# Turning a local attention's sums on VectorE in the main loop instead of on TensorE between the output products

## The chip, the cores and the metric

The kernel runs on one core of a Trainium2 chip. The metric is the time of one execution on the device, in microseconds. The core has five engines that run side by side, each through its own list of instructions in the order in which they were written: TensorE (PE in the profile, its weight loads PEld), VectorE (DVE), ScalarE (ACT), GpSimd (POOL) and SyncE (SP), whose queue issues the DMA transfers. An instruction waits on semaphores until what it needs is there, and everything behind it on its engine waits too.

## The reference

Two attentions over the same input of 2048 rows by 448 features, 16 heads of 28, mixed by a gate per row. Shortened:

```python
g = sigmoid((x * gate_w).sum(-1, keepdims=True))
a = local(x, A_wqkv) @ A_wo      # each row looks at rows s, s-2, ..., s-14
b = full(x, B_wqkv) @ B_wo       # softmax over all 2048 rows
return g * a + (1 - g) * b
```

All in float32. To keep that precision at TensorE's faster float32 rate, the kernel writes each operand as a rounded part and a remainder (hi and lo) and adds three products: hi by hi, hi by lo, lo by hi.

## The kernel before

Rows are spread so that partition p holds rows 16p to 16p+15; "j" counts these 16.

First come the projections (q, k, v of both attentions). Then the main loop: 256 steps, 16 units (4 groups of four heads by 4 blocks of 512 queries) of 16 key tiles. In each step `scores` issues twelve score products (three terms for each of four heads) and two exponentials of 128x1024 on ScalarE; `do_av` then issues the products with V for the step before. Into the same steps is woven a search ahead for the largest score of each later query: three products of 512 keys a step (`s0`, `s1`, `s2`), whose maxima VectorE takes in two instructions, one over one bank (`s0`), one over two (`s1`, `s2`). The scores' banks rotate among three two-bank tiles: the tile that `s1` and `s2` fill in one step holds the third and the fourth head's scores in the next. The order of the products in a step is the string

```python
WITH = "10 20 s0 11 21 30 00 12 22 31 01 s1 s2 32 02".split()
```

in which "30" is the first term of the third head, the first product that needs that tile. The search has a head start from the projections and ends at step 234; in the last 21 steps there are no maxima.

The local attention runs beside it in 8 chunks of two heads, on GpSimd (products and sums), VectorE (reductions) and ScalarE (exponentials). It is not written in order: `item` puts each piece into a list with a key, a cost and its needs, each need with a lag in steps, and `issue` takes from an engine's list, in each step, what is due, as long as the engine's estimated lateness `late` plus the cost stays under a limit; for VectorE the limit is `DLIM`, 0.6 before. Each step takes 0.4 off VectorE's lateness while there are maxima. A reduction of local scores (`a_reduce`) has cost 0.32, those of the softmax 0.35. VectorE's items of a step are issued behind the step's two maxima.

The sum of a chunk is stored by rows into `oa_scr` (one transfer of 128x16x56). When all lists are empty, `a_done` sets off the first loads for the output products. These are 16 tiles of 128 rows. A tile multiplies 128 rows of both attentions' sums (seven slices of 128 features) with the output weights: 21 products of 448 columns (12 for the first tile, whose first nine are issued in the last step of the main loop). The full attention's sums are stored by feature and already split, so they load ready for use. The local sums come by row: `op_t` turns four 128x128 squares on TensorE for the tile that follows, and `op_split` splits them from the bank, on ScalarE and VectorE. Beside the first tiles runs the end of the full attention's last unit (`fin_...`, the list `steps`): sums stored and loaded, inverted, spread, multiplied, split, stored.

Of the kernel before, what the change touches and what calls it, by code (L numbers as in the profile page):

```python
# [8 lines left out]
F32 = mybir.dt.float32  # L9
# [16 lines left out]
def gated_mix_kernel(ctx: ExitStack, tc: tile.TileContext, xT, xn, gw, wA, wB, woAB, out):  # L26
# [9 lines left out]
    a_prev = [t[:, 0:S, :].rearrange("c (p j) e -> c p j e", j=NJ) for t in a_scr]  # L36
    oa_scr = dram.tile([128, NJ, D], F32, name="oa_scr")
    on_hi = dram.tile([D, S], F32R, name="on_hi")
# [134 lines left out]

    def max_parts(u):
# [8 lines left out]
        nc.gpsimd.tensor_tensor(out=t[:, 16:32], in0=v, in1=t[:, 0:16].bitcast(F32), op=ALU.subtract)  # L183
        return t
# [399 lines left out]
    for nme in ("k", "v"):  # L584
        for i in range(2):
            t = a1.tile([128, HALO + NJ, 56], F32, name=f"{nme}t{i}")
            kvt[nme, i] = t
    qt, Lt, oat, lst, prods = {}, {}, {}, {}, {}

# [26 lines left out]
    def a_softmax(c, i):  # L616
# [23 lines left out]
        else:  # L640
# [3 lines left out]
                [128, W, NJ * 2]), op=ALU.mult)  # L644

    def a_av(c, w, part):
        if part == 0:
# [31 lines left out]
    for c in range(8):  # L679
        c0 = CH * c - 5 * (c == 7)  # L680
        for nme in "qkv":
            item("sp", c0 if nme != "v" else c0 + 18, ("ld", nme, c), 0,
                 [(("s", c - 2, 7), 3)] if nme != "v" else [(("a", c - 2, 7, 1), 3)],
                 lambda c=c, nme=nme: a_load(c, nme))
        for w, o in enumerate((0, 2, 5, 8, 11, 14, 17, 20)):
            back = (c, w - 4) if w > 3 else (c - 1, w + 4)
            item("pool", c0 + o, ("s", c, w), 3.15 + 0.5 * (NR[c, w] == 1),
                 [(("ld", "k", c), 4), (("ld", "q", c), 4), (("a", c - 3, 7, 0), 0), (("s", c, w - 1), 0)]
                 + ([(last(*back), 0)] if back in NR else []), lambda c=c, w=w: a_score(c, w))
            for i in range(NR[c, w]):  # L690
# [3 lines left out]
        for i, (eng, o, cost, lag) in enumerate((("pool", 22, 0.68, 2), ("dve", 23, 0.35, 3), ("dve", 23.5, 0.35, 0),  # L694
                                                 ("pool", 25, 0.68, 1), ("act", 26, 0.3, 3), ("dve", 27, 0.35, 1),
                                                 ("dve", 27.5, 0.35, 0), ("dve", 27.8, 0.36, 0),
                                                 ("pool", 28, 0.9, 1))):
            item(eng, c0 + o, ("m", c, i), cost, [(last(c, 7) if i == 0 else ("m", c, i - 1), lag)],
                 lambda c=c, i=i: a_softmax(c, i))
        n = 0  # L700
        for w in range(W):
            for part in ((0,) if w == 0 else (0, 1)):
                item("pool", CH * c + 30 + 1.4 * n, ("a", c, w, part), 1.65 if part == 0 else 2.05,
                     [(("m", c, 8), 0), (("ld", "v", c), 4),
                      (("a", c, w - 1, 1 if w > 1 else 0) if part == 0 else ("a", c, w, 0), 0)],
                     lambda c=c, w=w, part=part: a_av(c, w, part))
                n += 1
    for q in lists.values():
        q.sort(key=lambda x: x[0])
# [22 lines left out]
    WO_AT = OP0 + 8  # L732
    A_START, DLIM, LOOK = 5, 0.6, 40

# [28 lines left out]

    oaT, onT = {}, {}

    def op_load_a(j):
        t = mtile("oal")
        nc.sync.dma_start(t[:, :D], oa_scr[:, j, :])
        oaT[j] = t

# [11 lines left out]

    def op_t(j):
        t = oaT[j]
        for k in range(4):
            n = 128 if k < 3 else 64
            writes(side["t"], nc.tensor.transpose(side["t"][0:n, 128 * k:128 * k + 128], t[:, 128 * k:128 * k + n], ident))  # L787

    def op_split(j):
        b, jj = divmod(j, 4)  # L790
        bank = side["t"]
        cs = slice(128 * jj, 128 * jj + 128)
        hi, lo = mtile("oah").bitcast(F32R), mtile("oalo").bitcast(F32R)
        th, tl = on_tiles(b)[0]
        nc.scalar.activation(hi[:, :384], bank[:, :384], AF.Copy)
        nc.scalar.activation(th[0:64, cs], bank[0:64, 384:512], AF.Copy)
        nc.vector.tensor_tensor(out=lo[:, :384], in0=bank[:, :384], in1=hi[:, :384].bitcast(F32), op=ALU.subtract)
        nc.vector.tensor_tensor(out=tl[0:64, cs], in0=bank[0:64, 384:512], in1=th[0:64, cs].bitcast(F32),
                                op=ALU.subtract)
        oaT[j] = (hi, lo)  # L800

    TERMS = ((0, 0), (0, 1), (1, 0))

    def op_mm(j, bank, ks, first=False, last=False):
        b, jj = divmod(j, 4)
        for k in ks:
            for i, (a, c) in enumerate(TERMS):
                src = oaT[j][a][:, 128 * k:128 * k + 128] if k < 3 else onT[b][k - 3][a][:, 128 * jj:128 * jj + 128]
                writes(bank, nc.tensor.matmul(bank[:, :D], src, wo[c][k],  # L809
# [89 lines left out]
    accs = []  # L899
    side = {}  # L900
# [36 lines left out]
    def scores(u, kt, cur):  # L937
# [9 lines left out]
        for tok in WITH if k else ALONE:  # L947
# [13 lines left out]
            if t == 2 and a in "20":  # L961
                if len(exps) < 8:
                    probs.append(pair("P"))
                p = probs[len(exps) % 8]
                e = nc.scalar.activation(p, one if a == "2" else mine, AF.Exp, scale=SCALE).ins  # L965
                for o in exps[-8:-7]:
                    tc.declare_no_dep(e, o, query=mybir.DependencyQuery.ANY_SYNC,
# [7 lines left out]
    for u in range(NU):  # L975
        g, b = divmod(u, NB)
        for kt in range(NJ):
# [18 lines left out]
            if finished:  # L996
                v = finished.pop(0)
                t = max_parts(v)
# [60 lines left out]
```

## Time and profile before

| | |
|---|---|
| median of 3 runs | 910.9 us (910.88 to 911.29) |
| the profiled execution | 911.58 us, span 909.8 us from first to last instruction |
| granted TensorE clock | 1.000 |
| busy, share of the span | PE 99%, PEld 60%, DVE 80%, ACT 71%, POOL 70% |
| main loop | from about 255 us to 831 us |
| output products after it | from about 831 us to the end |

The profile has one execution, on the one core. Busy time of TensorE is modelled from pipelined products, so that 99% does not mean that it could go no faster. A row of the order of time has the start, the length, the engine, the line, the operation, what it writes and reads, how many of the kind stand in a row, and in brackets how long the engine was idle before and what ended it; lengths of instructions in a row overlap a little.

### The profile page before, as it was taken

To read this page: it belongs to the slowest core of one execution; us is meant where nothing else is said; L and a number is where in the kernel's file an instruction comes from. 1 tells how busy PE (TensorE), PEld (TensorE's weight loads), DVE (VectorE), ACT (ScalarE), POOL (GpSimd) and SP (SyncE) were. 2 spreads that over 40 slices of the span, in tenths; PEclk is the share of its full clock that TensorE was granted. 3 is DMA by queue.
4 is the path that set the end of the run, shared out by engine and by line. 5 is a ranking of instruction groups with operands and counts; after the bars stand their busy time and mean duration, and the time that the engine had idled before them with its cause. 6 is when DMAs were issued, how large, how long until landed. Compare 5 with 4: busy or idle time off the path is not lost.

```text
span 909.8 us, 20654 instructions
## 1 busy us (share of the span) xinstructions
PE 901.1 (99%) x8390; PEld 547.1 (60%) x8390; DVE 731.8 (80%) x934; ACT 649.3 (71%) x797; POOL 640.0 (70%) x505
## 2 busy tenths in 40 slices
PE   9999999999999999999999999999999999999998
PEld 6799999999954444444444444444444444336887
DVE  5588999999979999999999999999999988411221
ACT  6456434343378898898988898988989888995211
POOL 2389846564468659999999999999999987710100
PEclk9999999999999999999999999999999999999999
DMA  9877503459462341235235315421411321353672
GB/s 267 281 249 195 160 12 83 133 138 108 114 244 65 103 121 45 59 87 135 57 83 143 88 45 143 101 94 40 106 34 34 95 54 41 101 165 94 211 206 85
DMA packets 103960, 105.06 MB, mean 115 GB/s; under 512 B 64136, under 2 KB 73736, under 8 KB 103080
## 3 DMA queue, kind: packets, MB, share of 16 engines
q1 hardware_dynamic: 103720, 103.47, 41.4%
q8 instruction: 66, 1.08, 0.5%
q10 hardware_dynamic: 144, 0.26, 0.1%
q14 instruction: 30, 0.25, 0.1%
HBM read 62.72 MB, written 40.96 MB: 114 GB/s over the span
## 4 chain that ended last, share of the span: by engine, by line
PE 95%; DMA 2%; ACT 2%; DVE 1%; issue 0%; SPq 0%; ACTq 0%; DVEq 0%
PE T L960 29%; PE av L926 27%; PE r L300 15%; PE r L295 7%; PE T L809 6%; PE T L142 5%; PE r L142 4%; DMA oal<-oa_scr 1%; ACT P L965 1%; PE T L787 1%; DMA V<-in_xT 1%; DMA KH<-qk_hi 0%; ACT KH L748 0%; DVE res L818 0%; DVE xl L420 0%
## 5 line engine op out<-in xcount | busy, mean ns | idle before, releaser
L965 ACT ACTIVATE P<-T 128x1024 f32<-128x1024 f32 x512 | 496.9, 1025 | 57.4 <-PE T L960 56.1
L148 DVE TENSOR_REDUCE MX<-T 128x1 f32<-128x512 f32 x470 | 448.4, 957 | 32.1 <-PE T L142 13.1
L926 PE MATMUL av<-P,V 128*32 128x512 f32 x2048 | 272.7, 605 | 0.9 <-ACT osb L827 0.9
L960 PEld LDWEIGHTS T<-QH,KH 30*128 30x128 f32 x1024 | 92.7, 181 | 228.9 <-ACT P L965 197.8
L142 PE MATMUL T<-KH,QP 28*128 28x512 f32 x704 | 221.4, 460 | 0.1
L960 PE MATMUL T<-QH,KH 30*128 30x512 f32 x1024 | 212.0, 489 | 0.5 <-DMA QH<-nm 0.5
L164 DVE TENSOR_REDUCE MX<-r 128x2 f32<-128x1024 f32 x160 | 191.7, 1222 | 25.6 <-PE r L142 24.3
L960 PE MATMUL T<-QH,KL 28*128 28x512 f32 x1024 | 186.7, 394 | 0.0
L960 PE MATMUL T<-QL,KH 28*128 28x512 f32 x1024 | 185.4, 393 | 0.0
L604 POOL TENSOR_TENSOR prod<-qt,kt 128x896 f32<-128x896 f32 x64 | 135.3, 2114 | 7.9 <-DMA kt<-a_scr 4.5
L363 ACT ACTIVATE raw<-r 128x896 f32<-128x896 f32 (+1 forms) x64 | 58.9, 921 | 97.1 <-PE r L300 94.8
L659 POOL TENSOR_TENSOR oat<-oat,prod 128x896 f32<-128x896 f32 x56 | 118.1, 2109 | 2.7
L142 PEld LDWEIGHTS T<-KH,QP 28*128 28x128 f32 x704 | 86.0, 181 | 30.3 <-ACT P L965 22.0
L364 POOL TENSOR_TENSOR ast<-raw 128x448 f32<-128x448 f32 x48 | 55.3, 1153 | 58.1 <-ACT raw L363 49.2
L654 POOL TENSOR_TENSOR prod<-vt,L 128x896 f32<-128x896 f32 x56 | 95.4, 1704 | 0.4
L960 PEld LDWEIGHTS T<-QH,KL 28*128 28x128 f32 x1024 | 93.5, 183 | 0.7
L960 PEld LDWEIGHTS T<-QL,KH 28*128 28x128 f32 x1024 | 93.6, 184 | 0.0
L926 PEld LDWEIGHTS av<-P,V 128*32 128x32 f32 x2048 | 40.3, 108 | 76.4 <-issue 63.4
L300 PE MATMUL r<-wh,xh 64*128 64x448 f32 (+1 forms) x512 | 83.2, 363 | 0.0
L142 PE MATMUL r<-KH,QP 64*128 64x512 f32 x320 | 80.3, 392 | 1.0 <-DMA KH<-qk_hi 0.6
L300 PE MATMUL r<-wh,xl 64*128 64x448 f32 (+1 forms) x384 | 70.7, 364 | 0.0
L609 POOL TENSOR_TENSOR prod<-prod 128x448 f32<-128x448 f32 x64 | 65.5, 1023 | 5.0
(109 smaller groups left out, 1074.3 us busy)
## 6 DMA issues: line engine op xcount, KB each, us to landing
a_scr<-ast SPq DMA_DIRECT2D x24, 448.0 KB
qk_hi<-qkh SPq DMA_DIRECT2D x24, 256.0 KB
qk_lo<-qkh SPq DMA_DIRECT2D x24, 256.0 KB
rbc<-rs SPq DMA_DIRECT2D x64, 64.0 KB
QP<-qk_hi SPq DMA_DIRECT2D x64, 56.0 KB
KL<-qk_lo SPq DMA_DIRECT2D x16, 224.0 KB
QH<-qk_hi SPq DMA_DIRECT2D x64, 56.0 KB
QL<-qk_lo SPq DMA_DIRECT2D x64, 56.0 KB
```

The source lines that it names most:

```text
L142: nc.tensor.matmul(bank, qhis[u][h % 2][r, 128 * qs:128 * qs + 128], KH[u // NB % 3][r, 512 * kc:512 * kc + 512], start=True, stop=True)
L148: i = nc.vector.tensor_reduce(MX[:, n % NMX:n % NMX + k], bank, axis=X, op=ALU.max)
L164: nc.vector.tensor_reduce(m, PM[k], axis=X, op=ALU.max)
L295: nc.tensor.matmul(bank, ws[c][rows, k, t[4]:t[4] + 128], x, start=first, stop=last)
L300: nc.tensor.matmul(bank[:, 0:cols], x, ws[c][rows, k, 0:cols], start=first, stop=last)
L604: nc.gpsimd.tensor_tensor(out=p, in0=qt[c], in1=kvt["k", c % 2][:, HALO - DIL * w:HALO - DIL * w + NJ, :], op=ALU.mult)
L609: nc.gpsimd.tensor_tensor(out=lo, in0=lo, in1=hi, op=ALU.add)
L654: nc.gpsimd.tensor_tensor(out=dst.rearrange("p j (h d) -> p j h d", d=DH), in0=kvt["v", c % 2][:, HALO - DIL * w:HALO - DIL * w + NJ, :].r ...
L659: nc.gpsimd.tensor_tensor(out=oat[c], in0=oat[c], in1=oat[c, w], op=ALU.add)
L926: nc.tensor.matmul(av[32 * h:32 * h + 32, :], V[:, kt, 4 * g + h, :], tiles_[h], start=(kt == 0), stop=(kt == NJ - 1), skip_group_check=True)
L960: nc.tensor.matmul(bank[a], (KH[g % 3], KH[g % 3], KL[g % 2])[t][r, ks], (qh, ql, qh)[t][r, :], start=(t == 0), stop=(t == 2))
L965: e = nc.scalar.activation(p, one if a == "2" else mine, AF.Exp, scale=SCALE).ins
```

## The change

The local sums are turned on VectorE, which transposes each 32x32 square of a tile where it stands. The last sum of a chunk is written into one of two tiles `ow` of 64 columns for each j (56 and 8 of zeros). Four new items of VectorE a chunk, `a_turn`, cost 0.33 each, turn 128x256 each into the tile `tw`. Eight transfers then store it by feature (`oa_scr` is now [448, 2048]), which puts the squares where they belong. The three tiles come out of the pool of two-bank buffers, so the probabilities have five instead of eight.

The output products then load the local sums as they load the others, a slice of 128 features by 512 columns, and split it once a block of four tiles: `op_split` on ScalarE and VectorE, for the first block on VectorE alone, within the last steps of the main loop. `op_t` and its bank are gone.

Around it: `DLIM` is 0.8 instead of 0.6, the last chunk is due 12 steps earlier instead of 5, two lags of GpSimd's items are 2 instead of 1, and the small subtraction behind the search's maxima on GpSimd is issued a step later.

```diff
-    oa_scr = dram.tile([128, NJ, D], F32, name="oa_scr")
+    oa_scr = dram.tile([D, S], F32, name="oa_scr")
...
+        low = lambda: nc.gpsimd.tensor_tensor(out=t[:, 16:32], in0=v, in1=t[:, 0:16].bitcast(F32), op=ALU.subtract)
+        if later:
+            later(low)
...
-            nc.gpsimd.tensor_tensor(out=oat[c], in0=oat[c], in1=oat[c, w], op=ALU.add)
-            if w == W - 1:
-                stored[0] = now[0] + 4
-                at("end", stored[0], lambda: nc.sync.dma_start(oa_scr[:, :, 56 * c:56 * c + 56], oat[c]))
+            nc.gpsimd.tensor_tensor(out=ows[c % 2][:, :, 0:56] if w == W - 1 else oat[c], in0=oat[c], in1=oat[c, w], op=ALU.add)
+
+    def a_turn(c, i):
+        if not tw:
+            tw.append(wide("tw"))
+        r = slice(4 * i, 4 * i + 4)
+        nc.vector.transpose(tw[0][:, r, :].rearrange("p j e -> p (j e)"), ows[c % 2][:, r, :].rearrange("p j e -> p (j e)"))
+        if i == 3:
+            stored[0] = now[0] + 2
+            for a in range(4):
+                for f in (0, 32):
+                    n = min(32, 56 - f)
+                    at("end", stored[0] + a // 2 - 1, lambda a=a, f=f, n=n: nc.sync.dma_start(
+                        oa_scr[56 * c + f:56 * c + f + n, :].rearrange("f (j p) -> f j p", j=NJ)[:, :, 32 * a:32 * a + 32],
+                        tw[0][32 * a:32 * a + n, :, f:f + 32]))
...
-        c0 = CH * c - 5 * (c == 7)
+        c0 = CH * c - 12 * (c == 7)
...
+        for i in range(4):
+            item("dve", CH * c + 53 + i, ("t", c, i), 0.33,
+                 [(("a", c, W - 1, 1), 3) if i == 0 else (("t", c, i - 1), 1)]
+                 + ([(("t", c - 1, 3), 4)] if c else []), lambda c=c, i=i: a_turn(c, i))
...
-    A_START, DLIM, LOOK = 5, 0.6, 40
+    A_START, DLIM, LOOK = 5, 0.8, 40
...
-            at("end", st + 1 + k, lambda k=k: op_load_b(0, k))
-        at("end", st + 5, lambda: (op_load_a(0), op_load_a(1)))
+            at("end", st + 1 + k, lambda k=k: (op_load_a(0, k), op_load_b(0, k)))
+            at("dve", st + 4 + k, lambda k=k: op_split(0, k, nc.vector.tensor_copy))
...
+    def op_split(b, k, rounded=None):
+        raw = raws.pop((b, k))
+        hi, lo = oa_tiles(b)[k]
+        if rounded:
+            rounded(hi, raw)
+        else:
+            nc.scalar.activation(hi, raw, AF.Copy)
+        nc.vector.tensor_tensor(out=lo, in0=raw, in1=hi.bitcast(F32), op=ALU.subtract)
...
     def op_tile(j, behind):
         bank = accs[j % 2]
-        b = j // 4
+        b, k = divmod(j, 4)
         if j:
             op_mm(j, bank, (0, 1), first=True)
-        if j + 2 < NJ:
-            op_load_a(j + 2)
-        if j + 1 < NJ:
-            op_t(j + 1)
-            op_split(j + 1)
-        if j < 12:
-            op_load_b(b + 1, j % 4)
+        if b < 3:
+            op_load_a(b + 1, k)
+            op_load_b(b + 1, k)
+            if k:
+                op_split(b + 1, k - 1)
         for f in behind:
             f()
         op_mm(j, bank, (2, 3, 4, 5, 6) if j else (3, 4, 5, 6), last=True)
+        if b < 3 and k == 3:
+            op_split(b + 1, 3)
         op_out(j, bank, j % 2)
...
-                if len(exps) < 8:
+                if len(exps) < 5:
...
-                lag = 2 if v < NU - 1 else 1
+                lag = 3 if v < NU - 1 else 1
...
-            if st == NJ * NU - 2:
-                side["t"] = T1
-                op_t(0)
-                op_split(0)
```

Two places show what moves. The first is VectorE's list in the main loop, early in the local attention's work. L148 are the maxima, over one bank (128x1) and over two (128x2), the last of a step; behind it stand the planner's items, L614 before and L619 after, both the reduction of local scores. Before:

```order
235 L148 TENSOR_REDUCE MX<-T_3266 128x2
236 L614 TENSOR_REDUCE L<-prod 128x16
237 L148 TENSOR_REDUCE MX<-T_3274 128x1
238 L148 TENSOR_REDUCE MX<-T_3262 128x2
239 L614 TENSOR_REDUCE L<-prod 128x16
240 L148 TENSOR_REDUCE MX<-T_3274 128x1
```

After:

```order
226 L148 TENSOR_REDUCE MX<-T_3262 128x2
227 L619 TENSOR_REDUCE L<-prod 128x16 x2
228 L148 TENSOR_REDUCE MX<-T_3274 128x1
229 L148 TENSOR_REDUCE MX<-T_3266 128x2
230 L619 TENSOR_REDUCE L<-prod 128x16
231 L148 TENSOR_REDUCE MX<-T_3274 128x1
```

Where each step had one reduction between its maxima and the next step's, some steps now have two.

A later piece of VectorE's list after the change has the first of the new transposes (L676, from `ow` into `tw`), one of them in a step alone and one ahead of a reduction:

```order
363 L148 TENSOR_REDUCE MX<-T_3266 128x2
364 L676 STREAM_TRANSPOSE tw<-ow 128x256
365 L148 TENSOR_REDUCE MX<-T_3274 128x1
366 L148 TENSOR_REDUCE MX<-T_3262 128x2
367 L676 STREAM_TRANSPOSE tw<-ow 128x256
368 L619 TENSOR_REDUCE L<-prod 128x16
369 L148 TENSOR_REDUCE MX<-T_3274 128x1
```

They stand where the reductions stand, between two steps' maxima.

The second place is TensorE's list at the end of the main loop: L926 (before) and L946 (after) are the products with V, L787 the transposes of the local sums `oal`, L809 (before) and L832 (after) the output products. Before:

```order
3123 L809 MATMUL T_3270<-KH_152,oalo 128x448
3124 L926 MATMUL av<-P,V 32x512 x4
3125 L787 MATMUL T_3274<-ident,oal 128x128 x3
3126 L787 MATMUL T_3274<-ident,oal 64x128
3127 L809 MATMUL T_3270<-KH_152,onhi_10373 128x448
```

After:

```order
3121 L832 MATMUL T_3270<-KH_152,oalo_10522 128x448
3122 L946 MATMUL av<-P,V 32x512 x4
3123 L832 MATMUL T_3270<-KH_152,onhi_10443 128x448
```

The transposes between the products with V and the output products are gone, here and in each tile that follows.

More of the change, by code (lines that the diff above doesn't have):

```diff
@@ L170, in gated_mix_kernel, with max_parts @@
     halves = [0, 0]
-    def max_parts(u):
+    def max_parts(u, later=None):
         m = sp.tile([128, 16], F32, name="m")
@@ L182, in max_parts @@
         nc.scalar.activation(v, m, AF.Copy, scale=-1.0)
-        nc.gpsimd.tensor_tensor(out=t[:, 16:32], in0=v, in1=t[:, 0:16].bitcast(F32), op=ALU.subtract)
+        low = lambda: nc.gpsimd.tensor_tensor(out=t[:, 16:32], in0=v, in1=t[:, 0:16].bitcast(F32), op=ALU.subtract)
+        if later:
+            later(low)
+        else:
+            low()
         return t
@@ L587, in gated_mix_kernel @@
             kvt[nme, i] = t
+    ows, tw = [], []
     qt, Lt, oat, lst, prods = {}, {}, {}, {}, {}
@@ L644, in a_softmax, with wide @@
                 [128, W, NJ * 2]), op=ALU.mult)
+    def wide(name):
+        return pair(name).rearrange("p a b -> p (a b)").rearrange("p (j e) -> p j e", j=NJ)
     def a_av(c, w, part):
+        if len(ows) <= min(c, 1):
+            ows.append(wide("ow"))
+            nc.gpsimd.memset(ows[-1][:, :, 56:64], 0.0)
         if part == 0:
@@ L704, in gated_mix_kernel @@
                      [(("m", c, 8), 0), (("ld", "v", c), 4),
-                      (("a", c, w - 1, 1 if w > 1 else 0) if part == 0 else ("a", c, w, 0), 0)],
+                      (("a", c, w - 1, 1 if w > 1 else 0) if part == 0 else ("a", c, w, 0), 0)]
+                     + ([(("t", c - 2, 3), 0)] if c > 1 and w == W - 1 and part else []),
                      lambda c=c, w=w, part=part: a_av(c, w, part))
                 n += 1
+        for i in range(4):
+            item("dve", CH * c + 53 + i, ("t", c, i), 0.33,
+                 [(("a", c, W - 1, 1), 3) if i == 0 else (("t", c, i - 1), 1)]
+                 + ([(("t", c - 1, 3), 4)] if c else []), lambda c=c, i=i: a_turn(c, i))
     for q in lists.values():
@@ L762, in gated_mix_kernel, with oa_tiles, op_load_a @@
         at("act", WO_AT + 5 + k, lambda k=k: split_wo(k))
[L764 to L769, printed above, removed]
+    oaT, onT, raws = {}, {}, {}
+    def oa_tiles(b):
+        if b not in oaT:
+            oaT[b] = [[oP["2"].tile([128, 512], F32R, tag=f"oa{p}{k}", name=f"oa{p}{k}") for p in ("hi", "lo")]
+                      for k in range(3)]
+        return oaT[b] + [[t[0:64] for t in on_tiles(b)[0]]]
+    def op_load_a(b, k):
+        n = 128 if k < 3 else 64
+        raws[b, k] = mtile("oar")[0:n]
+        nc.sync.dma_start(raws[b, k], oa_scr[128 * k:128 * k + n, 512 * b:512 * b + 512])
+    def op_split(b, k, rounded=None):
[3 more added lines that the diff above has]
+            rounded(hi, raw)
+        else:
+            nc.scalar.activation(hi, raw, AF.Copy)
+        nc.vector.tensor_tensor(out=lo, in0=raw, in1=hi.bitcast(F32), op=ALU.subtract)
     def on_tiles(b):
@@ L781, in op_load_b @@
             dma_r(t[p0:p0 + n], src[r0:r0 + n, 512 * b:512 * b + 512])
[L783 to L800, printed above, removed]
     TERMS = ((0, 0), (0, 1), (1, 0))
@@ L807, in op_mm @@
             for i, (a, c) in enumerate(TERMS):
-                src = oaT[j][a][:, 128 * k:128 * k + 128] if k < 3 else onT[b][k - 3][a][:, 128 * jj:128 * jj + 128]
+                src = (oaT[b][k] if k < 3 else onT[b][k - 3])[a][:, 128 * jj:128 * jj + 128]
                 writes(bank, nc.tensor.matmul(bank[:, :D], src, wo[c][k],
@@ L961, in scores @@
             if t == 2 and a in "20":
-                if len(exps) < 8:
+                if len(exps) < 5:
                     probs.append(pair("P"))
-                p = probs[len(exps) % 8]
+                p = probs[len(exps) % 5]
                 e = nc.scalar.activation(p, one if a == "2" else mine, AF.Exp, scale=SCALE).ins
-                for o in exps[-8:-7]:
+                for o in exps[-5:-4]:
                     tc.declare_no_dep(e, o, query=mybir.DependencyQuery.ANY_SYNC,
@@ L997, in gated_mix_kernel @@
                 v = finished.pop(0)
-                t = max_parts(v)
+                t = max_parts(v, (lambda f: at("end", st + 1, f)) if v < NU - 1 else None)
                 late["dve"] += 0.3
                 turned = {}
-                lag = 2 if v < NU - 1 else 1
+                lag = 3 if v < NU - 1 else 1
                 at("dve", st + lag, lambda t=t, w=turned: w.update(r=max_turn(t)))
```

5 lines of the change are left out of this document (2 added, 3 removed).

## The prediction

> **What bounds the kernel now.** I read the page first (the chain that ended last), then the busy times by stage, then the order of time on each engine for a few steps of the main loop and of the output products, and the groups of instructions for prices.
>
> The page's chain, and three of the stages in the windows view (start:end, length, then busy PE, PEld, DVE, ACT, POOL, the granted clock, DMA share and GB/s): the main loop, the steps at its end in which no maxima are left, and the output products.
>
> ```profile
> PE 95%; DMA 2%; ACT 2%; DVE 1%; issue 0%; SPq 0%; ACTq 0%; DVEq 0%
> ...
> 550.00:600.00 50.00, 50.00 (x517) 20.82 (x518) 47.42 (x68) 44.52 (x50) 48.76 (x35) 1.00 0.44 113
> ...
> 808.00:826.00 18.00, 18.00 (x183) 6.61 (x176) 0.00 (x0) 17.34 (x20) 2.55 (x2) 1.00 0.47 141
> 826.00:910.00 84.00, 79.31 (x427) 69.49 (x425) 16.88 (x41) 18.69 (x46) 2.80 (x3) 1.00 0.51 152
> ```
>
> The chain is TensorE almost alone, at the full clock. That is not the whole story of the main loop: VectorE is busy 47.42 of 50 us there, and nothing in 808 to 826. So VectorE work costs nothing at the end and may cost something in the loop. How much is read from the loop itself, VectorE first (start, length, what, count, idle time before it in brackets), then TensorE's first products of each step and the ones on the bank that VectorE has to free.
>
> ```profile
> 601.29 1.94 DVE L148 TENSOR_REDUCE MX<-T 128x1 f32<-128x512 f32 x2 [0.25 <-PE T L960]
> 603.15 0.38 DVE L614 TENSOR_REDUCE L<-prod 128x16 f32<-128x224 f32 x1
> 603.57 1.90 DVE L148 TENSOR_REDUCE MX<-T 128x1 f32<-128x512 f32 x2
> 605.39 0.38 DVE L614 TENSOR_REDUCE L<-prod 128x16 f32<-128x224 f32 x1
> 605.75 2.03 DVE L148 TENSOR_REDUCE MX<-T 128x1 f32<-128x512 f32 x2
> 608.02 1.92 DVE L148 TENSOR_REDUCE MX<-T 128x1 f32<-128x512 f32 x2 [0.24 <-PE T L960]
> 609.85 0.38 DVE L614 TENSOR_REDUCE L<-prod 128x16 f32<-128x224 f32 x1
> 610.30 1.91 DVE L148 TENSOR_REDUCE MX<-T 128x1 f32<-128x512 f32 x2
> ```
>
> ```profile
> 603.00 0.50 PE L960 MATMUL T<-QH,KH 30*128 30x512 f32 x2
> 603.29 0.49 PE L960 MATMUL T<-QH,KH 30*128 30x512 f32 x1
> 605.17 0.50 PE L960 MATMUL T<-QH,KH 30*128 30x512 f32 x2
> 605.53 0.50 PE L960 MATMUL T<-QH,KH 30*128 30x512 f32 x2
> 607.44 0.50 PE L960 MATMUL T<-QH,KH 30*128 30x512 f32 x2
> 607.83 0.50 PE L960 MATMUL T<-QH,KH 30*128 30x512 f32 x2
> 609.99 0.49 PE L960 MATMUL T<-QH,KH 30*128 30x512 f32 x1
> ```
>
> Two things are to be seen. The pairs of maxima end at 603.23, 605.47, 607.78 and 609.94 (start plus length); a score product starts at 603.29, 605.53, 607.83 and 609.99, each time 0.05 or 0.06 us later. It is the third head's, which writes the two-bank tile that the second maximum has just read. So VectorE releases TensorE in every one of these steps: a maximum that ends later starts that product later, and the row of products behind it. And VectorE has little room: from 601.29 to 610.30 are four steps, 9.01 us, 2.25 each; a pair of maxima holds the engine 1.82 (603.57 to 605.39), one reduction of the local scores 0.36 (605.39 to 605.75). One fits: 2.18, with 0.07 over. Two make 2.54, 0.29 too much.
>
> **Part one, the output products (gain).** The transposes stand in TensorE's row, between output products.
>
> ```profile
> 849.54 0.60 PE L787 MATMUL T<-ident,oal 128*128 128x128 f32 x4
> ...
> 853.86 0.36 PE L809 MATMUL T<-KL,oah 128*128 128x448 f32 x1
> 854.06 0.37 PE L809 MATMUL T<-KH,oalo 128*128 128x448 f32 x1
> 854.27 0.60 PE L787 MATMUL T<-ident,oal 128*128 128x128 f32 x4
> ...
> 864.36 0.63 PE L787 MATMUL T<-ident,oal 128*128 128x128 f32 x4 [0.47 <-DMA oal<-oa_scr]
> ...
> 874.42 0.63 PE L787 MATMUL T<-ident,oal 128*128 128x128 f32 x4 [0.19 <-DMA oal<-oa_scr]
> ```
>
> A tile lasts 4.73 (849.54 to 854.27). It has 21 products, one every 0.205 (853.86 to 854.06): 4.30. So the four transposes cost 0.43, fifteen times in this stage: 6.5 us. The waits for `oal` go with them, 0.47 and 0.19. The first four stand in the main loop's last step but one, and ScalarE's split of them too:
>
> ```profile
> 826.59 0.50 ACT L795 ACTIVATE oah<-T 128x384 fp32r<-128x384 f32 x1
> 826.96 0.27 ACT L796 ACTIVATE onhi<-T 64x128 fp32r<-64x128 f32 x1
> 827.25 1.94 ACT L965 ACTIVATE P<-T 128x1024 f32<-128x1024 f32 x2
> ...
> 855.45 0.62 ACT L860 ACTIVATE onhi<-on 128x512 fp32r<-128x512 f32 x1
> ```
>
> The exponentials follow the split without a gap: without transposes and split they can start about as much earlier as TensorE's 0.43, so 0.4. Sum: 6.5 + 0.7 + 0.4 = 7.6 us.
>
> What comes instead is hidden. Block 0 is loaded in the four steps after the local branch has ended and split by VectorE (eight instructions of 128x512, some 0.6 us each if they take what ScalarE's last row takes) in the stretch in which it does nothing; without that cover it would be 5 us. The splits of the later blocks, one of 512 columns each on ScalarE and VectorE per tile, stand on engines that are busy 19 and 17 of 84 us. What can come late is the last load of a block: it is issued in the block's last tile behind the store of the tile before, about 1.0 us in (a copy of 0.6 and an issue of 0.4), and its split is needed after nine products of the next tile, 4.30 + 9 x 0.205 = 6.15 in. Less a copy and a subtraction of 0.6 each, the load has 3.9 us. How long a load takes under way is bounded by this pair (SyncE's queue), with 864.36 above:
>
> ```profile
> 859.06 0.38 SPq L768 DMA_DIRECT2D oal<-oa_scr  x1
> ...
> 862.34 3.52 SPq L99 DMA_DIRECT2D on_lo<-onlo  x4
> ```
>
> Issued at 859.06, its reader went at 864.36: at most 5.3 us, 1.4 too long, at three boundaries 4.2 us at worst; at best nothing. The only boundary with such traffic before it is the one behind tile 7, which follows the eight stores whose last four hold the queue 3.52 us, so I take 0.5. The part's net: -7.1 us (-7.6 to -3.4).
>
> **Part two, the main loop (loss).** The change puts 32 transposes of 128x256 into VectorE's list, and to make room it raises the lateness up to which the planner issues VectorE's items from 0.6 to 0.8. At 0.32 a reduction by its own costs, 0.6 held it to one item a step nearly always; 0.8 lets two through. The order of the instructions shows it: between two pairs of maxima stands never more than one of the planner's items before; now 46 of the steps with maxima have two: 31 two of L619's reductions, 8 two halves of a softmax reduction, 6 a transpose and a reduction, 1 a reciprocal and a reduction. Another 21 have a transpose alone.
>
> Prices come from these rows (mean ns behind the busy time):
>
> ```profile
> L614 DVE TENSOR_REDUCE L<-prod 128x16 f32<-128x224 f32 x128 | 47.6, 372 | 0.0
> L188 DVE STREAM_TRANSPOSE nms<-nmt 128x32 f32<-128x32 f32 x16 | 3.2, 202 | 2.3 <-POOL nmt L183 2.3
> ```
>
> A transpose of 128x256 is not in the trace. Its lower bound is the reduction of 128x224, 0.37; its upper bound eight of the 128x32 ones, 1.6. It streams about as many columns as the reduction and I take 0.40. Alone in a step it fits (2.25 - 1.82 = 0.43): nothing. [...]
>
> A second item pushes the maxima by 0.29. What of it reaches the end? Upper bound: all, since the product starts 0.05 behind the maximum. TensorE can take a little back: with the bank free early a step is 2.17 (603.00 to 605.17), with the wait 2.27 (605.17 to 607.44), so some 0.07 in the step after. Lower bound: what ScalarE's odd jobs cost, which push the exponentials likewise.
>
> ```profile
> 574.79 1.94 ACT L965 ACTIVATE P<-T 128x1024 f32<-128x1024 f32 x2
> 576.62 0.63 ACT L860 ACTIVATE onhi<-on 128x512 fp32r<-128x512 f32 x1
> 577.14 1.94 ACT L965 ACTIVATE P<-T 128x1024 f32<-128x1024 f32 x2
> 579.23 1.94 ACT L965 ACTIVATE P<-T 128x1024 f32<-128x1024 f32 x2 [0.15 <-PE T L960]
> 581.05 0.60 ACT L827 ACTIVATE osb<-av 128x512 f32<-128x512 f32 x1
> 581.57 1.94 ACT L965 ACTIVATE P<-T 128x1024 f32<-128x1024 f32 x2
> 583.86 1.94 ACT L965 ACTIVATE P<-T 128x1024 f32<-128x1024 f32 x2 [0.35 <-PE T L960]
> ```
>
> Two jobs hold it 0.52 each (576.62 to 577.14, 581.05 to 581.57); against the idle 0.35 of a plain step that is 0.34 too much in all. The four steps from 574.79 to 583.86 took 9.07, against 9.01 above: 0.06, a sixth. But ScalarE has idle time to catch up in, and VectorE with one item a step has 0.07. So I go by the nearer row, the product's start: 0.29 - 0.07 = 0.22 a step, 46 x 0.22 = 10.1 us (from 46 x 0.05 = 2.3 to 46 x 0.29 = 13.3).
>
> Edits that I cost at nothing. Five probability buffers for eight: the exponential of a step reuses what the product of at least two steps earlier read, and that product stands ahead of this step's scores on TensorE, for which the exponential waits anyway. The GpSimd subtraction of the maxima, moved a step on: the negated maxima of a block of queries are read many steps later, and for the last block nothing moves. 64 small stores for 8 on SyncE's queue: they are issued one and two steps after the last transpose of a chunk, so the queue waits for no engine, and next to nothing in the loop waits for SyncE. GpSimd's order with the last chunk earlier: it ends the local branch one step sooner (240 for 241).
>
> **The sum.** -7.1 + 10.1 = +3.0 us. The profiled execution took 911.58 us (span 909.8 and 1.8 around it), the median of the runs is 910.9; on the median: 913.9 us.
>
> **The rivals.**
>
> *The loop swallows the second item: faster.* The two-step chain through ScalarE and the rotating banks may have slack that the row of starts hides, as ScalarE's jobs suggest. Place: the steps with two items. It decides at 7.1 / 46 = 0.15 us a step: below that the change gains. At the lower bound of 0.05 the loop loses 2.3 and the time is 910.9 - 7.1 + 2.3 = 906.1. For it: the sixth above. Against: the four starts 0.05 behind the maxima. Chance 0.33.
>
> *The transposes are dear: slower still.* [...] Against it: the 128x32 transpose takes only 0.20. Chance 0.10. [...]
>
> *The block boundaries stall.* All three loads come 1.4 late: 4.2 in place of 0.5, 917.6. Against: the two waits shown are the only ones of the stage for a load. Chance 0.05.
>
> *The forecast*, between 0.15 and 0.29 a step: 910.7 to 917.1. Chance 0.52.
>
> **How the numbers follow.** 0.2% is 1.8 us, about what a measurement of this kernel tells from none. Slower by more needs a price over (7.1 + 1.8) / 46 = 0.19 a step: 0.43 of the forecast's 0.52, with the two slower rivals 0.58. Faster by more needs one under (7.1 - 1.8) / 46 = 0.12: 0.28 of the first rival's 0.33. Within it lies the rest of both, 0.09 and 0.05. The likeliest case's own range is 910.7 to 917.1; the range that holds 8 in 10 leaves out the far end of the first rival and the dear transposes: 905.0 to 919.5.
>
> **What would show it.** In the profile after: no transposes on TensorE and a tile of output products at 4.30; the stage from the last scores some 7 us shorter; the L619 pairs on VectorE with the next pair of maxima ending 0.3 later than in a plain step, and the third head's product 0.05 behind it; the main loop's steps at 2.25 + 10.1 / 230 = 2.29 on the mean. Wrong: steps of 2.25 in spite of the pairs (first rival), transposes of over 0.43 (second), TensorE waiting at the first k of a block (third).

## The result and the profile after

The changed kernel takes 919.6 us (median of 4 runs, 918.8 to 920.2) against 911.1 on the same chip: a ratio of 1.0091 (95% interval in brackets, here and below: [1.0074, 1.0109]). The forecast was 913.9 (905.0 to 919.5) and slower. So the sign held and the size did not: +8.5 us for +3.0, at the upper end of the range. The profiled execution took 919.04 us, its span is 917.2 against 909.8, +7.4.

The page's chain that ended last, and stages in the windows view of the changed kernel (start:end, length, busy PE, PEld, DVE, ACT, POOL, the granted clock, DMA share, GB/s):

```profile
PE 90%; DMA 4%; SPq 3%; ACT 2%; issue 1%; DVE 0%; POOL 0%; ACTq 0%; POOLq 0%
...
550.00:600.00 50.00, 50.00 (x510) 20.96 (x514) 47.29 (x70) 44.43 (x50) 47.14 (x34) 1.00 0.40 100
...
819.80:825.00 5.20, 0.00 (x0) 0.00 (x0) 0.00 (x0) 1.30 (x2) 1.86 (x2) 0.67 0.15 50
825.00:830.00 5.00, 4.71 (x30) 1.87 (x30) 0.00 (x0) 3.09 (x4) 0.67 (x1) 0.50 0.55 129
```

The chain was TensorE almost alone; now DMA and SyncE's queue hold 7% of it (a share of the chain's length, not of the time lost). In the main loop VectorE is as busy as before (47.29 of 50), nothing like 10 us more. But at 819.80, six steps from the main loop's end, TensorE stands still for over 5 us, and behind that it runs at half its clock.

How the 7.4 us divide, by the starts of the steps' first exponentials in both traces (step 8 at 273.9, 232 at 777.1, 248 at 812.5, 255 at 827.3 before):

| | change, us | forecast |
|---|---|---|
| up to step 8, where the code is the same | -0.6 | |
| steps 8 to 232, the loop with maxima | +2.4 | +10.1 |
| steps 248 to 255 | +8.0 | -0.4 |
| from step 255 to the end, the output products | -2.4 | -6.7 |

The three terms are each several us from their forecast, in different directions. The first line is no effect: in the profiled executions of the changed kernel and of the experiments the start lies -0.6 to +2.7 us from before's, also with code that is before's there. What causes this was not looked into; effects are therefore read inside the loop, and medians of many runs stand beside them.

**The stand at 820.** SyncE's queue, GpSimd, ScalarE and TensorE of the changed kernel, in the order of time (start, length, what, count, idle time before it and what ended it):

```profile
794.69 3.01 SPq L682 DMA_DIRECT2D oa_scr<-tw  x4
...
801.37 2.90 SPq L682 DMA_DIRECT2D oa_scr<-tw  x4
804.38 0.53 SPq L855 DMA_DIRECT2D rs<-osb  x1
805.01 0.38 SPq L802 DMA_DIRECT2D oar<-oa_scr  x1
...
813.32 0.32 SPq L868 DMA_DIRECT2D rs<-finv  x1
819.00 1.72 SPq L873 DMA_DIRECT2D rbc<-rs  x4
```

```profile
822.40 1.26 POOL L879 TENSOR_TENSOR on<-osb,rbc 128x512 f32<-128x512 f32 x1 [11.90 <-DMA rbc<-rs]
```

```profile
823.70 0.63 ACT L883 ACTIVATE onhi<-on 128x512 fp32r<-128x512 f32 x1 [5.57 <-POOL on L879]
```

```profile
825.29 0.79 PE L980 MATMUL T<-QH,KH 30*128 30x512 f32 x2 [5.62 <-ACT P L985]
```

Read upwards: TensorE waits for an exponential, which stands on ScalarE behind the split of unit 14's sums; that waits for GpSimd, GpSimd for `rbc`, and `rbc` is the last link of a chain (`rs<-osb`, `fsum<-rs`, `rs<-finv`, `rbc<-rs`; the second is issued at 806.72) that stands in SyncE's queue behind the eight stores and among the loads of block 0. In before the same chain, with one store ahead of it, was in time:

```profile
797.52 0.59 SPq L662 DMA_DIRECT2D oa_scr<-oat  x1
798.21 1.11 SPq L832 DMA_DIRECT2D rs<-osb  x1
...
805.79 0.33 SPq L845 DMA_DIRECT2D rs<-finv  x1
...
810.45 1.72 SPq L850 DMA_DIRECT2D rbc<-rs  x4
```

```profile
813.98 1.28 POOL L856 TENSOR_TENSOR on<-osb,rbc 128x512 f32<-128x512 f32 x1 [8.22 <-DMA rbc<-rs]
```

```profile
816.25 0.63 ACT L860 ACTIVATE onhi<-on 128x512 fp32r<-128x512 f32 x1
```

The split at 816.25 had no wait, but GpSimd, whose product ended at 815.26, was only 1.0 us ahead of it. That is the margin which the forecast did not look for.

**The output products.** TensorE's rows in tile 8, SyncE's queue before it, and ScalarE's split:

```profile
878.24 0.47 PE L832 MATMUL T<-KH,onhi 128*128 128x448 f32 x1 [2.84 <-ACT onhi L810]
...
880.13 0.58 PE L832 MATMUL T<-KH,onhi 128*128 128x448 f32 x1
880.51 0.58 PE L832 MATMUL T<-QP,onhi 128*128 128x448 f32 x1
```

```profile
868.12 2.53 SPq L99 DMA_DIRECT2D on_hi<-onhi  x4
870.75 3.57 SPq L99 DMA_DIRECT2D on_lo<-onlo  x4
874.42 0.36 SPq L844 DMA_DIRECT2D out<-res  x1
874.84 0.46 SPq L802 DMA_DIRECT2D oar<-oa_scr  x1
```

```profile
877.55 0.63 ACT L810 ACTIVATE onhi<-oar 64x512 fp32r<-64x512 f32 x1 [4.22 <-DMA oar<-oa_scr]
```

TensorE waits 2.84 us for the split of the last load of block 2, which is issued at 874.84 behind eight stores that held the queue 6.1 us. Then, from 879.8 to 882.7, the products come every 0.37 us instead of 0.205.

**The main loop.** VectorE in some steps of the changed kernel, with one and with two reductions:

```profile
480.13 0.67 DVE L619 TENSOR_REDUCE L<-prod 128x16 f32<-128x224 f32 x2
480.72 1.81 DVE L148 TENSOR_REDUCE MX<-T 128x1 f32<-128x512 f32 x2
...
496.50 1.81 DVE L148 TENSOR_REDUCE MX<-T 128x1 f32<-128x512 f32 x2
498.23 0.38 DVE L619 TENSOR_REDUCE L<-prod 128x16 f32<-128x224 f32 x1
498.53 2.00 DVE L148 TENSOR_REDUCE MX<-T 128x1 f32<-128x512 f32 x2
```

Two reductions hold the engine 0.59 (480.13 to 480.72), one 0.30 (498.23 to 498.53), and a pair of maxima that has nothing to wait for 1.73 (496.50 to 498.23). So a step with two reductions needs 1.73 + 0.59 = 2.32 against the loop's 2.25: 0.07 too much, not 0.29.

### The profile page after: what moved, and what is told of

The parts are those of the page before. It is cut to its first block, busy times and chain, and to the rows that moved or that the text cites. A ratio compares the mean times of both kernels' runs of the same rounds, so it can differ in the third digit from the quotient of the medians.

```text
span 917.2 us, 20553 instructions
## 1 busy us (share of the span) xinstructions
PE 900.8 (98%) x8326; PEld 541.5 (59%) x8326; DVE 734.7 (80%) x954; ACT 646.9 (71%) x777; POOL 640.1 (70%) x507
## 4 chain that ended last, share of the span: by engine, by line
PE 90%; DMA 4%; SPq 3%; ACT 2%; issue 1%; DVE 0%; POOL 0%; ACTq 0%; POOLq 0%
PE T L980 29%; PE av L946 26%; PE r L304 15%; PE T L832 6%; PE r L299 6%; PE r L142 4%; PE T L142 4%; SPq L99 1%; ACT P L985 1%; DMA oar<-oa_scr 1%; DMA onlo<-on_lo 1%; DMA rs<-finv 1%; DMA onhi<-on_hi 1%; SPq L682 1%; DMA raw<-in_wB 0%
## 5 line engine op out<-in xcount | busy, mean ns | idle before, releaser
L148 DVE TENSOR_REDUCE MX<-T 128x1 f32<-128x512 f32 x470 | 442.1, 954 | 34.0 <-PE T L142 14.4
L946 PE MATMUL av<-P,V 128*32 128x512 f32 x2048 | 274.4, 608 | 0.9 <-ACT osb L850 0.9
L980 PE MATMUL T<-QH,KH 30*128 30x512 f32 x1024 | 214.9, 491 | 5.8 <-ACT P L985 5.8
L670 POOL TENSOR_TENSOR oat<-oat,prod 128x896 f32<-128x896 f32 x48 | 101.2, 2108 | 2.0
L946 PEld LDWEIGHTS av<-P,V 128*32 128x32 f32 x2048 | 40.5, 108 | 79.2 <-issue 66.5
L614 POOL TENSOR_TENSOR prod<-prod 128x448 f32<-128x448 f32 x64 | 65.6, 1024 | 5.0
```

The lines of the kernel that those rows point to most:

```text
L148: i = nc.vector.tensor_reduce(MX[:, n % NMX:n % NMX + k], bank, axis=X, op=ALU.max)
L614: nc.gpsimd.tensor_tensor(out=lo, in0=lo, in1=hi, op=ALU.add)
L670: nc.gpsimd.tensor_tensor(out=ows[c % 2][:, :, 0:56] if w == W - 1 else oat[c], in0=oat[c], in1=oat[c, w], op=ALU.add)
L946: nc.tensor.matmul(av[32 * h:32 * h + 32, :], V[:, kt, 4 * g + h, :], tiles_[h], start=(kt == 0), stop=(kt == NJ - 1), skip_group_check=True)
L980: nc.tensor.matmul(bank[a], (KH[g % 3], KH[g % 3], KL[g % 2])[t][r, ks], (qh, ql, qh)[t][r, :], start=(t == 0), stop=(t == 2))
```

## The experiments

Two questions stood against each other. Does SyncE's queue make the loss, by what stands in it ahead of unit 14's chain, or do VectorE's pairs, as forecast? And is a second item on VectorE, or a second transpose, paid in full, or swallowed by the loop?

**The split four steps later (changed kernel).** The list of steps at which the last pieces of unit 14 are issued; its split moves from step 250 to 254 with the two pieces behind it; in the queue nothing ahead of the chain moves:

```diff
-        l = {NU - 3: (1, 2, 5, 6, 9, 12, 13, 15), NU - 2: (1, 2, 5, 6, 8, 10, 10, 12)}.get(
+        l = {NU - 3: (1, 2, 5, 6, 9, 12, 13, 15), NU - 2: (1, 2, 5, 6, 8, 14, 14, 15)}.get(
```

> The changed kernel with the last three pieces of unit 14's end (fin_hi, fin_lo, fin_store) due at steps 254, 254 and 255 instead of 250, 250 and 252; nothing else. Theory Q: the 5.6 us for which TensorE stands at step 249 is ScalarE standing at fin_hi, whose sums arrive late because SyncE's queue is full; due four steps later ScalarE does not stand, TensorE does not idle and its clock stays at 1.00. The stretch from step 248 to 255 falls from 22.7 us to the 14.7 of before, so the time falls by about 8 us, to 911 to 912. Rival P (the forecast's own): the loss sits in the main loop's pairs of reductions, and this edit gives under 1 us.

912.3 us, ratio 1.0003 [0.999, 1.0015]. The chain is as late as in the changed kernel, but ScalarE reaches the split only when its data are there:

```profile
821.12 1.72 SPq L873 DMA_DIRECT2D rbc<-rs  x4
```

```profile
827.99 0.63 ACT L883 ACTIVATE onhi<-on 128x512 fp32r<-128x512 f32 x1
```

Steps 248 to 255 take 14.1 us, against 22.7 in the changed kernel and 14.7 before. The whole +8.0 was that one wait in ScalarE's list, with the slow clock behind it. The loop with maxima keeps its loss, +2.3.

**Eight stores for one (kernel before).** Only the last chunk's store is cut in eight; nothing else of the change is in this kernel.

```diff
-                at("end", stored[0], lambda: nc.sync.dma_start(oa_scr[:, :, 56 * c:56 * c + 56], oat[c]))
+                for i in range(8 if c == 7 else 1):
+                    p = slice(16 * i, 16 * i + 16) if c == 7 else slice(0, 128)
+                    at("end", stored[0], lambda p=p: nc.sync.dma_start(oa_scr[p, :, 56 * c:56 * c + 56], oat[c][p]))
```

> The kernel before with one part of the change alone: the last chunk's local sums stored in eight transfers (16 partitions each) instead of one, at the same step. Theory Q: eight issues take some 0.4 to 0.7 us each on SyncE's queue, so unit 14's chain behind them starts 3 to 5 us later; fin_hi had about 1 us to spare (its input was ready at 815.3, it ran at 816.3), so ScalarE and TensorE stand 2 to 4 us, and the time rises by 2 to 5 us, to 913 to 916. Rival L: the chain is late because of the loads of block 0 that the change puts ahead of it in the queue; then eight stores alone cost under 0.5 us.

916.7 us, ratio 1.0049 [1.0036, 1.0063]. The kernel before gets the same stand from the stores alone, a smaller one (its queue, then TensorE, then two half microseconds of the windows view with the granted clock third from the end):

```profile
800.51 5.25 SPq L664 DMA_DIRECT2D oa_scr<-oat  x8
806.18 0.54 SPq L834 DMA_DIRECT2D rs<-osb  x1
...
816.46 1.72 SPq L852 DMA_DIRECT2D rbc<-rs  x4
```

```profile
822.82 0.50 PE L962 MATMUL T<-QH,KH 30*128 30x512 f32 x2 [1.98 <-ACT P L967]
```

```profile
823.00:823.50 0.50, 0.50 (x8) 0.38 (x10) 0.00 (x0) 0.50 (x1) 0.20 (x1) 0.74 0.53 119
826.50:827.00 0.50, 0.50 (x12) 0.25 (x4) 0.00 (x0) 0.00 (x0) 0.00 (x0) 0.85 0.64 201
```

Steps 248 to 255 are 3.6 us longer for 1.98 us of stand: the rest is the clock, at half speed from about 823.2 to 826.6.

**The loads of block 0 five steps later (changed kernel).** The eight stores stay where they are.

```diff
-            at("end", st + 1 + k, lambda k=k: (op_load_a(0, k), op_load_b(0, k)))
-            at("dve", st + 4 + k, lambda k=k: op_split(0, k, nc.vector.tensor_copy))
+            at("end", st + 6 + k, lambda k=k: (op_load_a(0, k), op_load_b(0, k)))
+            at("dve", st + 9 + k, lambda k=k: op_split(0, k, nc.vector.tensor_copy))
```

> The changed kernel with the loads of block 0 for the output products issued five steps later (246 to 249 instead of 241 to 244) and split five steps later; the eight stores stay where they are. It parts the two things that stand ahead of unit 14's chain on SyncE's queue: with the stores alone (e2) TensorE stood 2.0 us and lost 3.6 in all in steps 248 to 252. Theory Q: stores and loads each have their part, so the stand falls from 5.6 to about 2 us and steps 248 to 255 from 22.7 to 18 to 19 us: time about 915. Rival: the loads have no part in it, then the stand stays at 5 us or more and the time at 919 to 920. Rival: the loads are all of it, then the stand goes.

912.0 us, ratio 0.9991 [0.9981, 1.0001]. Here the queue's theory, as I had sized it, fell: it left about 2 us of the stand to the stores, and steps 248 to 255 take 14.2 us, no stand at all. (This trace is of one execution, of 909.8 us; what the others lose up to the median of 912.0 it does not show.) With no load under way the chain runs through in half the time:

```profile
807.49 0.53 SPq L855 DMA_DIRECT2D rs<-osb  x1
811.49 0.34 SPq L868 DMA_DIRECT2D rs<-finv  x1
812.92 1.72 SPq L873 DMA_DIRECT2D rbc<-rs  x4
```

From `rs<-finv` to `rbc<-rs`, which waits for it to land, are 1.43 us here, 5.68 in the changed kernel (813.32 to 819.00) and 4.66 before. The five traces agree on one account. When the issue of `rbc` ends, counted from the start of step 240, and how long ScalarE then stands:

| | chain starts | `rbc` issued | ScalarE waits |
|---|---|---|---|
| before | 3.4 | 17.3 | 0 |
| before, eight stores | 8.4 | 20.4 | 1.9 |
| changed | 7.8 | 24.1 | 5.6 |
| changed, later blocks' loads early (below) | 7.8 | 25.0 | 6.7 |
| changed, block 0's loads later | 8.5 | 15.6 | 0 |

The wait is what `rbc` is later than before's 17.3, less 1.0 to 1.2: 3.1 gives 1.9, 6.8 gives 5.6, 7.7 gives 6.7. That is the 1.0 us of margin seen in before. The stores delay the chain's start by 4.4 us (7.8 - 3.4); the loads between its links stretch it from 7.1 (8.5 to 15.6) to 16.3 us. Before had its stretch too (13.9, with its own loads of block 0 between the links). So the lateness has two parts: the stores alone bring `rbc` from 17.3 to 20.4, and the rest of the change, with four loads of `oar` among the links, brings it to 24.1 (no run adds these four alone). The rival that the loads are all of it would fit this run alone; the stand with the eight stores in the kernel before speaks against it.

**The later blocks' loads two at a time (changed kernel).** The same loads, in the first two tiles of a block instead of in each of its four, and their splits ahead of the products of the tile.

```diff
-            op_load_a(b + 1, k)
+            if k < 2:
+                op_load_a(b + 1, 2 * k)
+                op_load_a(b + 1, 2 * k + 1)
...
-            if k:
-                op_split(b + 1, k - 1)
+            for i in ((), (0, 1), (2,), (3,))[k]:
+                op_split(b + 1, i)
...
-        if b < 3 and k == 3:
-            op_split(b + 1, 3)
```

> The changed kernel with the local sums' loads of a block issued two in each of the first two tiles of the block before (instead of one in each of four), and split one tile later at most (two, one, one), the last split ahead of the tile's products instead of behind. Theory: the wait of 2.84 us at the first product of tile 8 that needs the fourth slice, and the slow clock behind it, come from the last load of a block, issued at 874.84 behind the eight stores of unit 15; issued earlier it is there in time. The output products lose 4 to 4.5 us: time 915 to 916. Rival: the transfers as such are too slow in that stretch (the loads share the DMA engines with 960 KB a tile), then the wait moves and under 1 us is won.

917.5 us, ratio 1.0048 [1.0031, 1.0065], more than the 915 to 916 expected: the stand of the last steps is still in it, and steps 248 to 255 are 9.1 us longer than before in its trace, for 8.0 in the changed kernel's. From step 255 to the end are 75.2 us, against 80.2 in the changed kernel and 82.5 before: -7.3, which is what the forecast took for the gain. One wait is left there:

```profile
881.63 0.47 PE L832 MATMUL T<-KH,onhi 128*128 128x448 f32 x1 [0.22 <-DMA onhi<-on_hi]
```

So the transposes were worth their price, and the boundary behind tile 7 had eaten almost 5 us of it (80.2 - 75.2), not 0.5.

**The limit alone (kernel before, `DLIM` 0.8 for 0.6).** No transposes; 54 steps now have two of the planner's items, more than the changed kernel's 46.

> The kernel before with DLIM at 0.8 and nothing else: 54 of its steps with maxima then have two of the planner's reductions on VectorE, and the local branch ends at step 235 instead of 241. The forecast's price of 0.22 us a pair: +11.9 us between steps 8 and 232. The price read from the profile after the change (two reductions hold VectorE 0.59 and not 0.72, a pair of maxima 1.73 and not 1.82, so a step with two is 2.32 against 2.25): at most 54 x 0.08 = 4.3 us there, and 2.4 / 46 = 0.05 a pair gives 2.8. Total 913 to 915 by this price, 923 by the forecast's.

914.5 us, ratio 1.0029 [1.0017, 1.004]. Steps 8 to 232 are 2.1 us longer: 0.04 a step with two items, where the forecast's 0.22 would make 11.9. A pair costs that little without the rest of the change too.

**Each transpose twice (changed kernel).** A second transpose of the same 128x256 into a tile that nothing reads.

```diff
+    tx = mp.tile([128, 256], F32, name="tx")
...
+        nc.vector.transpose(tx, ows[c % 2][:, r, :].rearrange("p j e -> p (j e)"))
```

> The changed kernel with each of the 32 transposes issued a second time, into a tile that nothing reads; the planner does not know of the second. It measures what an excess on VectorE costs when it is larger than a pair's. Two transposes hold VectorE about 0.80 (0.40 each, from 500.44 to 500.85 in the profile after), with a pair of maxima at 1.73 a step of 2.53 against 2.25: 0.28 too much, 28 times in steps with maxima, 6 of them with a reduction on top. Theory V (VectorE releases TensorE, and what goes beyond the room is paid in full, the forecast's argument with the right sizes): steps 8 to 232 lose 28 x 0.28 + 6 x 0.3 = 9 to 10 us more than the 2.4 of the changed kernel. Rival L (the loop swallows most of it, as ScalarE's jobs suggested, a sixth passes): under 2 us more.

923.9 us, ratio 1.0128 [1.0112, 1.0144]. Steps 8 to 232 are 6.0 us longer than before, 3.6 more than the changed kernel's: between what the two theories gave. VectorE's rows:

```profile
575.68 0.43 DVE L677 STREAM_TRANSPOSE tw<-ow 128x256 f32<-128x256 f32 x1
576.03 0.40 DVE L678 STREAM_TRANSPOSE tx<-ow 128x256 f32<-128x256 f32 x1
576.36 1.78 DVE L148 TENSOR_REDUCE MX<-T 128x1 f32<-128x512 f32 x2
578.07 0.42 DVE L677 STREAM_TRANSPOSE tw<-ow 128x256 f32<-128x256 f32 x1
```

A transpose holds the engine 0.35 and 0.33, not its length of 0.43 or 0.40; with the maxima's 1.71 (576.36 to 578.07) a step needs 2.39, 0.14 over 2.25. The forecast's 21 steps with a transpose alone make 2.9, its 6 with a reduction beside it another 6 x 0.33 = 2.0; of these 4.9 us 3.6 were paid, three quarters. Of the pairs' 0.07 it was 0.05, about as much. So VectorE's excess does reach the end, mostly, as the forecast had it; the excess itself was taken too large.

**Both cures together (changed kernel).** The split of unit 14 later, and the later blocks' loads two at a time: the edits of the first and the fourth experiment.

> The changed kernel with both edits: the last three pieces of unit 14's end due at 254, 254 and 255 (as in e1), and the local sums' loads two a tile in the first two tiles of a block (as in e4). Theory: the two losses add up and so do their removals. From the traces: main loop, steps 8 to 232, +2.4 us against before; steps 248 to 255, -0.6 (e1); output products after step 255 75.2 (e4) against 82.5, -7.3. Sum -5.5: about 905.5 to 906.5, faster than both kernels. Rival: the transfers of the one stage collide with those of the other (unit 14's four late stores come just ahead of the first loads), and a wait of 2 us or more comes back at the first boundary: 908 or more.

906.6 us, ratio 0.9943 [0.9931, 0.9956]: faster than both kernels, each taken against before on its chip. The stretch in which the changed kernel stands, and the output products, in the windows view:

```profile
800.00:832.00 32.00, 31.10 (x298) 11.72 (x293) 7.21 (x13) 31.31 (x37) 2.79 (x3) 1.00 0.52 132
832.00:904.00 72.00, 69.02 (x342) 62.24 (x340) 13.12 (x21) 12.85 (x23) 2.81 (x3) 0.99 0.63 178
```

The clock is full, and against before the steps 8 to 232 stand at +2.6, 248 to 255 at -0.6, the end at -7.8: -5.8, the difference of the medians (906.6 to 912.4 on that chip).

## Why the prediction came out as it did

**The sign, for the wrong reason.** The forecast's loss was to come from VectorE's pairs. Most of the loss came from the queue instead, which the prediction cost at nothing; with the two waits behind the queue taken out, the same change is a gain of 5.8 us. That the sign held is luck.

**Edits costed at nothing: the step that failed.** "64 small stores for 8 on SyncE's queue: ... the queue waits for no engine, and next to nothing in the loop waits for SyncE." The first half is right. The second is wrong at the loop's end, for the last chunk: the chain of unit 14 goes through that queue four times, GpSimd waits for it, ScalarE for GpSimd, and every exponential for ScalarE. The loads of block 0, called hidden because VectorE splits them in idle time, stand in the same place. The step looked at who waits for the loads, not at what they stand in front of. It cost 8.0 us: 5.6 of stand, the rest the clock. The chain and its 1.0 us of margin were in the profile of before.

**Part two, the main loop: mis-sized.** +10.1 forecast, +2.4 measured; 0.05 a step instead of 0.22. The mechanism is right, since some three quarters of an excess are paid, but the hold times, 1.82 for the maxima and 0.36 for a reduction, were read at 603.57, 605.39 and 605.75, in steps that had time to spare. Taken singly, the first maximum of that pair holds 0.68 (603.57 to 604.25), that of the pair at 496.50 in the changed kernel 0.60 (to 497.10). A wait for a product inside the pair fits this, but no bracket shows it. Two items stood back to back in the profile of before as well, and I passed them over:

```profile
594.25 0.24 DVE L840 RECIPROCAL finv<-fsum 128x16 f32<-128x16 f32 x1
594.41 0.33 DVE L614 TENSOR_REDUCE L<-prod 128x16 f32<-128x224 f32 x1
594.66 1.86 DVE L148 TENSOR_REDUCE MX<-T 128x1 f32<-128x512 f32 x2
```

Here a reduction behind another item holds 0.25. The rival that the loop swallows the second item, at 0.05 a step, gave this term its right size. Its time, 906.1 for 910.9, is a gain of 4.8; without the two waits the kernel gains 5.8 (906.6 for 912.4).

**Transposes.** 0.40 forecast, 0.43 in the groups of the changed kernel, and the trace shows no engine that waited for one:

```profile
L676 DVE STREAM_TRANSPOSE tw<-ow 128x256 f32<-128x256 f32 x32 | 13.6, 430 | 0.1
```

What counts is the hold, 0.34 for 256 columns, beside 0.30 for the reduction's 224: the same per column, 1.3 ns. The rival of dear transposes is out: the hold is under the 0.43 that fits a step.

**Part one, the output products.** The gain of the removed transposes was right: -7.3 and -7.8 with the loads early. The block boundary behind tile 7 was named, with the eight stores that hold the queue, and priced at 0.5; it cost 2.84 of wait and 1.95 of slow products, most of them at half clock (0.50 to 0.55 from 879.5 to 883.0; fifteen from 878.24 to 883.27, 5.03 us instead of 15 x 0.205). In the other traces of the changed kernel that leave these loads as they are, the same wait is 1.92 (the split later), 1.18 (block 0's loads later) and 1.63 (each transpose twice). The rival put 1.4 on each of three boundaries by the time of a load under way. It was one boundary, and not the load but its place in the queue: issued at 874.84, it had landed by 877.55, 2.7 us later.

**What else was costed at nothing** (five probability buffers, the subtraction a step later, GpSimd's order) shows no cost of size. Steps 232 to 248, between the two losses, differ by less than 0.05 us, which speaks for the buffers. The other two lie in the loop with maxima, where no run takes them alone. There the changed kernel and its variants lose 0.2 to 0.6 us more than the limit alone does, with fewer pairs; why stays open.

## What to carry to other kernels

A transfer that nobody waits for can have a price in what stands behind it in its queue: here unit 14's chain started 4.4 us later behind the eight stores. Before calling it hidden, follow the queue to the next transfer with a waiter, and the waiter through its engine's own order, down to the engine on the path; the margin to ask for stands in the trace of before as the time by which the data were ready ahead of their reader.

Take an engine's hold from start to start in rows that follow an overdue instruction; the pair of maxima read in steps with time to spare held 1.82 here, behind an overdue instruction 1.73.

Where a late transfer makes an in-order engine stand, issuing the waiting instruction later can be worth as much as making the transfer earlier (here 912.3 and 912.0).

## What the runs showed of the hardware

The stands of TensorE cost more than their length, with the granted clock at half in or behind them: 8.6 us for 5.62 (22.7 - 14.1, the changed kernel and the split moved), 4.8 for 2.84, 3.6 for 1.98. The windows view of the changed kernel, in half microseconds (the granted clock is the third number from the end), at the fall and the return, for the stand at 820 and for the one at 875:

```profile
821.50:822.00 0.50, 0.00 (x0) 0.00 (x0) 0.00 (x0) 0.00 (x0) 0.00 (x0) 0.52 0.24 78
831.50:832.00 0.50, 0.50 (x5) 0.00 (x1) 0.00 (x0) 0.50 (x1) 0.00 (x0) 0.74 0.10 29
...
879.50:880.00 0.50, 0.50 (x3) 0.46 (x2) 0.00 (x0) 0.00 (x0) 0.00 (x0) 0.55 0.09 33
882.50:883.00 0.50, 0.50 (x3) 0.46 (x2) 0.00 (x0) 0.38 (x1) 0.00 (x0) 0.54 0.71 217
```

Taking each row's mean as a step from 1.0 to 0.5 or back, the clock is at half from 821.5 to 831.8, 10.2 us, and from 879.6 to 883.0, 3.4 us. With the eight stores in the kernel before it was 823.2 to 826.6, again 3.4. In both of the shorter stands, 1.98 and 2.84 us, the clock fell only after TensorE was at work again (823.2 behind 822.82, 879.6 behind 878.24). In the other traces the wait at tile 8 goes with these mean granted clocks of the profiled execution. With the split later, 1.92 us, it is 0.998, as one stretch of 3.4 us at half would make it (3.4 x 0.5 / 909.3 = 0.002); with block 0's loads later, 1.18 us, it is 1.000. With each transpose twice, 1.63 us, it is 0.994, which a stretch of 10.2 us as in the changed kernel would make by itself (10.2 x 0.5 / 920.2 = 0.006).

On the two rates of float32, in the kernel before: four transposes in plain float32, 512 columns together, cost TensorE 0.43 us, 0.84 ns a column; an output product of rounded parts came every 0.205 us for 448 columns, 0.46 ns.
